# Ten weight pairs instead of eight of the second half's second layer by seven products, with joins and weight differences in other slots

## The chip, the cores and the metric

The kernel runs on one core of one Trainium2 chip. The metric is device time in microseconds (us). Five engines work side by side, each with its own in-order queue: TensorE (PE in the profile; its weight loads are PEld), VectorE (DVE), ScalarE (ACT), GpSimd (POOL) and SyncE (SP), which here issues all DMAs. L893 is line 893 of the kernel.

## The reference

One layer norm feeds two branches, and both are added to the input. All values are float32.

```python
S, D, F = 2048, 576, 4608          # tokens, width, hidden width
xn = layernorm(x)
# A: 32 heads of 18, each token looks at itself and 7 earlier ones, 2 apart
q, k, v = split(xn @ wqkv)
o = softmax(q . k[pos - 2 w], w = 0..7) . v
# B: Dense -> Mish -> Dense
act = mish(xn @ w1 + b1)
y = act @ w2
out = x + o @ wo + y
```

## The kernel before

**Numbers.** Each float32 operand of a matrix product is split into a high part (a ScalarE copy to the type fp32r) and a low part (the rest, a subtraction on VectorE or GpSimd). A product is three matmuls: high by high, high by low, low by high.

**Halves, blocks, weight pairs.** The 2048 tokens are two halves of 1024 (`hf`), each half two blocks of 512 (`b`), each block four tiles of 128. The hidden width is 36 slices of 128; two slices make a weight pair `q`, 0 to 17. In the second half the slices are taken in the order `Q1`. `m1_part(hf, q, part)`, parts 0 to 5, computes the first layer of a weight pair for both blocks by seven products (lines 680 and 686), and `mish` makes the activations: an addition on VectorE where the product is a sum of two (L725), Mish on ScalarE (L726), a high copy (L731) and a low part on GpSimd (L732).

**The second layer, two forms.** In the first half `m2_pair` (L780) and in the second `m2_cols` (L893) multiply the activations of one weight pair with its two slices of w2 and add the result to the accumulators. One call is a chunk: two token tiles, two column halves of 288, 24 matmuls. A weight pair has four chunks, in the order of `CHUNKS`: block 1 twice, block 0 twice. Each of the four results of a chunk lies in one of the four PSUM banks called `out`, and VectorE adds it to its accumulator (L784, L896), which frees the bank.

The other form is used in the second half for weight pairs 1 to 2 x `OC`, two pairs at a time (`e`, from 0 to `OC` - 1). The two blocks of tokens and the two column halves make a 2 x 2 product, done by seven products instead of eight (Strassen and Winograd's scheme). `p_item(e, k)` is one of the seven, in the order `ORD` = P7, P4, P1, P5, P2, P6, P3; it has 24 matmuls (L872). Its left side is an activation or a sum of activations (`u_sum`, L814), split by `u_high` (L820) and `u_low` (L826); its right side is a quarter of w2 or a difference of quarters, kept in DRAM by the first half and brought by `p_fetch` (L840). For that the first half makes the differences T3, T1, T2, T4 of each such weight pair (`t_sum`, L301), splits them (`t_high` L307, `t_low` L312) and stores them (`t_keep`, L322 and L323). Each product has an accumulator of its own over all `e`, two tiles each (`accP1` to `accP7`); VectorE adds to it (L878). P2, P3, P4 and P5 start from the input x. When the last seven are done, `p_join` (L881, GpSimd) adds accumulators to each other, 14 additions of 128 x 576, so that P2, P3, P4 and P5 become the four quarters of the output, to which the remaining chunks add directly.

In the second half, position q of the order has weight pair `Q1[q]` = q + 1 (the last position has 0). The names of slots, `spot(1, q, i)`, and the table `early` go by position, so that `early[16]` and `early[17]` are the last two weight pairs. Positions 0 to 2 x `OC` hold their activations unsplit in buffers given by `raw_act`, since the sums are made of them; position 2 x `OC` is the first whose second layer goes by chunks, and `a_split` (L834, L835) splits what it holds.

**The order.** The program is a list `plan` of steps: attention projections, parts of `m1_part`, products, chunks, and at the end the output projection. `quad(hf, q)` writes one weight pair's steps; ten such steps of a pair are named by `spot(hf, q, i)`, i from 0 to 9. `before(i, fn)` hangs further work in front of step i. Engines get their instructions in exactly this order, and nothing is moved later.

**Attention** of a half is a generator of 73 steps: per pair of head groups four multiplies q by k on GpSimd (L539, two instructions) with a reduction on VectorE (L544), one softmax step, four multiplies by v (L577) with a reduction (L583). The reduction of a step is issued in the next step, so that GpSimd has time. After the last one VectorE transposes (L603) and SP stores to DRAM (L612). `cuts[hf]` lists the steps of the plan that carry an attention step. In the first half they follow from estimated costs at a spacing in `t`; in the second half from the table `early` (three slots a weight pair where products run, five else), cut off at 73, which today puts the last two of them on the first two of the final four chunks. Where a step is in `behind_adds` or `behind_next`, its reduction goes behind the additions of that step or the next.

**Other work in the queues.** The second half's part of the attention projection is also done by seven products; its weights (names beginning with z: `z_load` L385, `z_sum`, `z_high`, `z_low`, `z_keep`) are prepared in the first half in tiles of the pool `xn`, which has five and which the differences T use too. `wo_load`, `wo_sum`, `wo_keep_high` and so on prepare the output projection's weights in the second half. In the output projection (`wo_part`, L1076) each pair of token tiles is split by `o_split` (L924 to L955), the first of them during the last chunks, and VectorE adds the results (L1080).

Of the kernel before, what the change touches and what calls it, by code (L numbers as in the profile page):

```python
# [28 lines left out]
UQ = 4  # L29
PU = 2  # L30
CU = 2 * DH
OC = 4
Q1 = [*range(1, NP), 0]
HC = D // 2
EPS = 1e-5
# [4 lines left out]
def block_kernel(ctx: ExitStack, tc: tile.TileContext, x, wq, wo, w1, b1, w2, mask, out):  # L40
# [469 lines left out]
    behind_adds, behind_next, now = set(), set(), [0]  # L510
# [181 lines left out]
    def raw_act(q, b, j):  # L692
        if not rslot:
            for n in range(4):
                rslot["raw", n] = sb.tile([P, 5 * P], F32, tag="raw", bufs=4, name=f"ra{n}")
            for n in range(5):
                rslot["mn", n] = sb.tile([P, D], F32, tag="mn", bufs=5, name=f"rm{n}")
            for n in range(2):
                rslot["tt", n] = sb.tile([P, 4 * P], F32, tag="tt", bufs=2, name=f"rt{n}")
        tag, n = {(0, 0): (("raw", 0), ("raw", 1), ("raw", 2)), (1, 0): (("mn", 2), ("mn", 3), ("mn", 0), ("r3", 0)),  # L700
                  (0, 1): (("raw", 3), ("mn", 4), ("mn", 1)), (1, 1): (("tt", 0), ("tt", 1))}[b, j][q % {(1, 0): 4, (1, 1): 2}.get((b, j), 3)]
        if (tag, n) not in rslot:
            rslot[tag, n] = sb.tile([P, 2 * 432], F32, tag="r3", bufs=1, name="ra_r")
        rawact[q, b, j] = rslot[tag, n][:, 0:TB]
        owner[tag, n] = q, b, j
        where[q, b, j] = tag, n
        return rawact[q, b, j]
# [448 lines left out]
    at = {}  # L1156
# [26 lines left out]
    items = []  # L1183
# [172 lines left out]
    def spot(hf, q, i):  # L1356
        return at["s", hf, q, i]

    for q in range(NP):
        if q == 0:  # L1360
            i = at["q", 0, 3, 1, 0]
            ps_ = dict(raw=i - 3, sums=i - 1, wa=i, wc=i + 1, t0=i + 2, t1=i + 4)
        elif q == 1:
            i = at["q", 0, 3, 0, 0]
# [16 lines left out]
    for q in range(1, 2 * OC + 1):  # L1381
        i = spot(0, q, (3,2)[q > 1])
# [5 lines left out]
    i = spot(0, NP - 1, 0)  # L1388
# [5 lines left out]
    i = at["q", 1, 0, 1, 1]  # L1394
    for name, k, d in (("T2", 0, 0), ("T2", 1, 1), ("T3", 0, 2), ("B11", 0, 3), ("B11", 1, 4), ("B21", 0, 5),
                       ("B21", 1, 6), ("R2", 0, 7), ("T3", 1, 8), ("R3", 0, 9), ("T1", 0, 10), ("T1", 1, 10),
                       ("T4", 0, 11), ("T4", 1, 11), ("B22", 0, 11), ("B22", 1, 11)):
        before(i + d, lambda name=name, k=k: z_fetch(name, k))
    i = spot(0, 9, 4)
    for k in range(2):  # L1400
        for n, steps in enumerate((
# [4 lines left out]
            for kind, name in steps:  # L1406
                f = dict(l=z_load, s=z_sum, h=z_high, o=z_low, k=z_keep)[kind]
                d = 30 + 2 * n + (n >= 14) if k else 2 * n if n < 10 else (19, 20, 22, 23, 25, 26, 27)[n - 10]
                before(i + d, lambda f=f, name=name, k=k: f(name, k))
    for q in range(NP):  # L1410
        if q == 0:
            i = at["z", JB - 1, 0]
            ps_ = dict(wa=i - 7, t0=i - 6, t1=i - 5, wc=i - 4)
        elif q == 1:
            i = spot(1, 0, 0)
# [22 lines left out]
    J = 2 * OC + 1  # L1438
    for b in range(NB):
        for j in range(2):  # L1440
            before(spot(1, J, 0) + (2,3,1,2)[2 * b + j], lambda b=b, j=j: a_split(b, j))
    for n, (a, b) in enumerate((("P6", "P1"), ("P7", "P6"), ("P6", "P5"), ("P2", "P1"), ("P3", "P6"), ("P4", "P7"), ("P5", "P7"))):
        for pr in range(2):
            i = items[-2][2] + 1 + (0,1,2)[n] if n < 3 else at["p", 1, J + 0 - 1, n > 4, pr] + (1, 7, 1, 2)[n - 3]
            before(i, lambda a=a, b=b, pr=pr: p_join(a, b, pr))

    i = at["q", 0, 1, 1, 0]
# [3 lines left out]
    i = at["q", 0, 3, 1, 0]  # L1451
# [5 lines left out]
    i = at["q", 1, 0, 1, 1]  # L1457
    for n in range(8):
        c, k = divmod(n, 4)
        d = i + (0, 1, 3, 4, 6, 8, 10, 12)[n]  # L1460
        before(d, lambda c=c, k=k: s_step(1, c, k))
        d = max(d + 2, (at["q", 1, 1, 1, 2], at[("z", 1, 2)])[c] if k == 3 else 0)
# [4 lines left out]
    for n in range(0, JB, 2):  # L1467
        i = at["q", 0, 1, 0, n]
# [4 lines left out]
    for n in range(TJ):  # L1473
        i = spot(0, 2 + n, 2)
# [3 lines left out]
    i = spot(0, NP - 2, 0)  # L1478
# [7 lines left out]
    for n, (name, pr) in enumerate((name, pr) for name in ("P4", "P5", "P2", "P3") for pr in range(2)):  # L1486
        i = items[dict(P4=0, P5=2, P3=2, P2=3)[name]][2] + pr
# [2 lines left out]


    att = {}
    behind_adds.update((at["p", "x", OC - 1, 4], at["p", "x", 0, 4]))
    behind_next.add(at["m", 1, 10, 3])
    T = [0.0]
    for p_ in plan:
        T.append(T[-1] + p_[2])
# [15 lines left out]
    cuts = [[], []]  # L1513
    k = marks[0] - 1
    for n in range(steps - len(last_steps)):
        t = 6.111 * n
        k = next(k for k in range(k + 1, len(plan)) if T[k + 1] > t and ok[k])
        cuts[0].append(k)
    cuts[0] += last_steps
    early = {0: (8,), 1: (0, 2, 4, 6, 8), 2: (0, 4, 7), 3: (0, 3, 6), 4: (0, 4, 7), 5: (0, 3, 7), 6: (1, 4, 7),  # L1520
             7: (0, 4, 7), 8: (1, 4, 8), 9: (1, 3, 7)}
    for q in range(NP):
        cuts[1] += [spot(1, q, i) for i in early.get(q, (1, 3, 5, 7, 9))]
        if q == 2 * OC:
# [6 lines left out]
        for k in cuts[hf]:  # L1531
            before(k, lambda hf=hf: next(att[hf], None))

    i = spot(1, *(11,3))
    for k in range(4):
        before(i - 8 + 2 * k, lambda k=k: wo_load(k))
    for n in range(4):
        before(i + (0,2,4,6)[n], lambda n=n: wo_sum(n))
    for n, name in enumerate(("T3", "T1", "T2", "T4", "B11", "B21", "B22", "R", "D")):
        k = i + 10 + (2, 5, 10, 15, 20, 25, 30, 35, 40)[n]  # L1540
        if name == "R":
            before(k - 8, lambda: wo_rest(0))
        before(k, lambda name=name, n=n: wo_keep_high(name, n))
        before(k + 1, lambda name=name: wo_keep_low(name))
        before(k + 2, lambda name=name: wo_keep(name))
    i = spot(1, NP - 1, 0)
# [71 lines left out]
```

## Time and profile before

| | us |
|---|---|
| median of 3 runs (lowest to highest) | 1112.72 (1112.7 to 1113.13) |
| the profiled execution | 1113.35 |
| its span | 1111.6 |
| TensorE busy | 1101.6 |
| VectorE busy | 850.2 |
| GpSimd busy | 789.8 |
| ScalarE busy | 498.9 |

A page gives busy time by engine, the chain of work that ended last, and groups of instructions with their count, busy time, mean duration and the idle time of the engine in front of them. The timeline has a row for each group of equal instructions: start, length, engine, line, operation, tiles, count, and in brackets how long the engine was idle in front of it and who ended that. Matmuls are pipelined: neighbours overlap in these rows, so distances between starts are what counts. In the chain, rows are start, length, what. The windows view gives busy time and count of PE, PEld, DVE, ACT and POOL in a stretch, then clock, DMA share and GB/s. The last matmul of the first half's second layer (L780) starts at 545.5 us; the products (L872) start between 654.3 and 824.2; the second half's chunks (L893) start between 827.0 and 1053.8, and the output projection follows.

### The profile page before, as it was taken

How to read it: one execution, taken by the hardware profiler on the slowest of the kernel's cores; microseconds unless marked ns; L12 is line 12 of the kernel's file. 1: busy time of each engine (PE TensorE's matmuls, PEld its weight loads, DVE VectorE, ACT ScalarE, POOL GpSimd, SP SyncE). 2: the span in 40 equal slices, each digit the busy share in tenths (PEclk: the TensorE clock that was granted, in tenths of full speed). 3: DMA queues.
4: the chain of work that ended last, by engine and by line, in shares of the span. 5: the costliest groups of instructions: out<-in, count | busy, mean ns of one | idle time of the engine just before them, and what ended most of it. 6: DMA issues, size and time to landing. Idle time of an engine off the chain costs nothing.

```text
span 1111.6 us, 18209 instructions
## 1 busy us (share of the span) xinstructions
PE 1101.6 (99%) x6550; PEld 1014.5 (91%) x6550; DVE 850.2 (76%) x1367; ACT 498.9 (45%) x917; POOL 789.8 (71%) x639
## 2 busy tenths in 40 slices
PE   8999999999999999999999999999999999999998
PEld 7999899999999999999999888999888999999998
DVE  6359788888889888897656567877876677777786
ACT  5544655544454544555333354443432344343353
POOL 2479777766779688685788666666688976867542
PEclk9999999999999999999999999999999999999999
DMA  6899696868777768675598799656674657776674
GB/s 200 284 311 312 231 346 225 282 237 274 255 247 263 264 212 298 249 255 201 187 322 268 225 378 304 214 189 207 219 230 161 210 195 214 245 284 219 183 233 142
DMA packets 178270, 271.60 MB, mean 244 GB/s; under 512 B 53218, under 2 KB 120068, under 8 KB 178180
## 3 DMA queue, kind: packets, MB, share of 16 engines
q1 hardware_dynamic: 178180, 270.44, 72.3%
q8 instruction: 52, 0.85, 0.3%
q14 instruction: 38, 0.31, 0.1%
HBM read 160.39 MB, written 110.00 MB: 243 GB/s over the span
## 4 chain that ended last, share of the span: by engine, by line
PE 90%; DMA 4%; DVE 2%; POOL 1%; ACT 1%; SPq 1%; issue 1%; POOLq 0%; DVEq 0%
PE h L680 27%; PE po L780 21%; PE pq L348 11%; PE po L893 11%; PE po L872 6%; PE h L686 5%; PE o L1076 5%; PE z L446 3%; DMA acc<-in_x 1%; DMA kv<-kv_d 1%; DMA t<-kept_t 1%; DMA accP<-in_x 1%; SPq L612 1%; POOL act L732 1%; DMA pw<-kept_T 1%
## 5 line engine op out<-in xcount | busy, mean ns | idle before, releaser
L780 PEld LDWEIGHTS po<-w,act 128*128 128x128 f32 x1728 | 236.4, 188 | 6.0 <-POOL act L732 0.4
L780 PE MATMUL po<-w,act 128*128 128x288 f32 x1728 | 240.7, 295 | 0.1
L539 POOL TENSOR_TENSOR pr<-q,kv 128x576 f32<-128x576 f32 x128 | 197.3, 1566 | 8.1 <-DMA q<-q_d 4.9
L732 POOL TENSOR_TENSOR act<-c,act 128x512 fp32r<-128x512 f32 x81 | 107.4, 1327 | 128.5 <-ACT act L731 127.9
L577 POOL TENSOR_TENSOR pv<-L,kv 128x576 f32<-128x576 f32 x128 | 178.4, 1488 | 24.8 <-DVE L L570 19.9
L784 DVE TENSOR_TENSOR acc<-po,acc 128x288 f32<-128x288 f32 x288 | 119.5, 449 | 29.9 <-PE po L780 28.8
L348 PE MATMUL pq<-wq,xt 128*128 128x432 f32 x672 | 136.4, 361 | 1.1 <-ACT xt L81 1.1
L893 PEld LDWEIGHTS po<-w,act 128*128 128x128 f32 x960 | 130.9, 188 | 5.9 <-DVE accP L896 3.0
L893 PE MATMUL po<-w,act 128*128 128x288 f32 x960 | 133.3, 295 | 2.4 <-DVE accP L896 2.4
L348 PEld LDWEIGHTS pq<-wq,xt 128*128 128x128 f32 x672 | 125.0, 188 | 8.1 <-ACT xt L81 1.9
L726 ACT ACTIVATE c<-c,b1c 128x512 f32<-128x512 f32 x81 | 58.7, 725 | 140.9 <-DVE c L725 140.6
L680 PE MATMUL h<-xt,t 128*128 128x512 f32 x432 | 110.6, 391 | 0.7 <-DVE rt L725 0.7
L680 PE MATMUL h<-S,t 128*128 128x512 f32 x432 | 110.5, 391 | 0.0
L583 DVE TENSOR_REDUCE og<-pv 128x144 f32<-128x1152 f32 x64 | 85.9, 1345 | 23.9 <-POOL pv L577 23.8
L680 PE MATMUL h<-xt,wa 128*128 128x512 f32 x432 | 104.1, 390 | 0.0
L544 DVE TENSOR_REDUCE L<-pr 128x64 f32<-128x1152 f32 x64 | 85.8, 1342 | 23.3 <-POOL pr L539 23.2
L714 ACT COPY c<-h 128x512 f32<-128x512 f32 x81 | 47.4, 586 | 124.5 <-PE h L686 73.4
L680 PEld LDWEIGHTS h<-xt,wa 128*128 128x128 f32 x432 | 80.9, 188 | 17.0
L872 PEld LDWEIGHTS po<-pw,u 128*128 128x128 f32 x672 | 91.9, 188 | 3.8 <-DVE accP L878 1.3
L872 PE MATMUL po<-pw,u 128*128 128x288 f32 x672 | 94.1, 295 | 0.5 <-DVE accP L878 0.3
L680 PEld LDWEIGHTS h<-xt,t 128*128 128x128 f32 x432 | 79.1, 188 | 15.6 <-DVE rt L725 1.2
L896 DVE TENSOR_TENSOR accP<-po,accP 128x288 f32<-128x288 f32 x160 | 69.0, 452 | 31.7 <-PE po L893 29.0
(228 smaller groups left out, 1852.1 us busy)
## 6 DMA issues: line engine op xcount, KB each, us to landing
kv<-kv_d SPq DMA_DIRECT2D x64, 396.0 KB, 4.8
kept_t<-t SPq DMA_DIRECT2D x36, 512.0 KB, 4.8
t<-kept_t SPq DMA_DIRECT2D x36, 512.0 KB, 6.4
rw<-in_w SPq DMA_DIRECT2D x36, 320.0 KB, 4.8
kept_wa<-wa SPq DMA_DIRECT2D x18, 640.0 KB, 4.9
kept_w<-w SPq DMA_DIRECT2D x20, 576.0 KB, 4.2
wa<-kept_wa SPq DMA_DIRECT2D x18, 640.0 KB, 5.2
w<-kept_w SPq DMA_DIRECT2D x20, 576.0 KB, 4.1
```

The lines of the kernel that those rows point to most:

```text
L348: nc.tensor.matmul(pq[:, 0:432], XT[:, xi, tok], wt[wi][:, hl, 0:432], start=i == 0, stop=i == len(seq) - 1)
L539: nc.gpsimd.tensor_tensor(out=pr[:, x:x + hh], in0=q[:, j0 + x:j0 + x + hh, None, :].to_broadcast([P, hh, W, CU]), in1=win(kt, 0, CU, j0 + ...
L544: nc.vector.tensor_reduce(L[:, k, j0:j0 + hj].rearrange("p j w h -> p (j w h)"), pr.rearrange("p j w (h d) -> p (j w h) d", h=2), axis=AX, ...
L577: nc.gpsimd.tensor_tensor(out=pr[:, x:x + hj].rearrange("p j d w -> p j w d"), in0=L[:, k, x:x + hj, :, h:h + 1].to_broadcast([P, hj, W, DH]),
L583: nc.vector.tensor_reduce(og[:, c0:c0 + DH, :].rearrange("p d j -> p j d"), pr, axis=AX, op=ALU.add)
L680: nc.tensor.matmul(ph, wt[:, wl, wk * P:(wk + 1) * P], X[:, xs, :], start=first and i == 0, stop=last and i == len(seq) - 1, skip_group_ch ...
L732: nc.gpsimd.tensor_tensor(out=a[:, 1, :], in0=t, in1=a[:, 0, :].bitcast(F32), op=ALU.subtract)
L780: nc.tensor.matmul(po, acts[hf, q, b, j][:, al, tok], done["w2", hf, 2 * q + j][:, wl, c * HC:(c + 1) * HC], start=i == 0, stop=i == 5)
L784: nc.vector.tensor_tensor(out=t, in0=po, in1=t, op=ALU.add)
L872: nc.tensor.matmul(po, units[e, k, qq][:, al, tok], w[:, qq, wl, :], start=i == 0, stop=i == 5)
L893: nc.tensor.matmul(po, acts[hf, q, b, j][:, al, tok], done["w2", hf, 2 * q + j][:, wl, c * HC:(c + 1) * HC], start=i == 0, stop=i == 5)
L896: nc.vector.tensor_tensor(out=t, in0=po, in1=t, op=ALU.add)
```

## The change

`OC` becomes 5: weight pairs 9 and 10 go from chunks to a fifth set of seven products, and the first half prepares their weight differences. The joins get other slots, and P3 += P5 in front of the last product replaces P6 += P5; the sums are the same. One reduction loses its place behind additions. The preparation of the z weights, the attention steps of both halves and the output projection's weights get other slots, and one held activation another buffer.

```diff
@@ -29,7 +29,7 @@
-OC = 4
+OC = 5
@@ -698,7 +698,7 @@ raw_act
         tag, n = {(0, 0): (("raw", 0), ("raw", 1), ("raw", 2)), (1, 0): (("mn", 2), ("mn", 3), ("mn", 0), ("r3", 0)),
-                  (0, 1): (("raw", 3), ("mn", 4), ("mn", 1)), (1, 1): (("tt", 0), ("tt", 1))}[b, j][q % {(1, 0): 4, (1, 1): 2}.get((b, j), 3)]
+                  (0, 1): (("raw", 3), ("mn", 4), ("mn", 1)), (1, 1): (("tt", 0), ("tt", 1))}[b, j][3 if (q, b, j) == (2 * OC, 1, 0) else q % {(1, 0): 4, (1, 1): 2}.get((b, j), 3)]
@@ -1396,7 +1396,7 @@
-    i = spot(0, 9, 4)
+    i = spot(0, 10, 6)
     for k in range(2):
         for n, steps in enumerate((
...
                 f = dict(l=z_load, s=z_sum, h=z_high, o=z_low, k=z_keep)[kind]
-                d = 30 + 2 * n + (n >= 14) if k else 2 * n if n < 10 else (19, 20, 22, 23, 25, 26, 27)[n - 10]
+                d = 28 * k + (2 * n if n < 10 else (19, 20, 22, 23, 25, 26, 27)[n - 10])
@@ -1439,9 +1439,11 @@
-    for n, (a, b) in enumerate((("P6", "P1"), ("P7", "P6"), ("P6", "P5"), ("P2", "P1"), ("P3", "P6"), ("P4", "P7"), ("P5", "P7"))):
-        for pr in range(2):
-            i = items[-2][2] + 1 + (0,1,2)[n] if n < 3 else at["p", 1, J + 0 - 1, n > 4, pr] + (1, 7, 1, 2)[n - 3]
+    last = at["p", "x", OC - 1, 5]
+    for pr in range(2):
+        for a, b, i in (("P3", "P5", last), ("P6", "P1", last + 1), ("P7", "P6", last + 3),
+                        ("P2", "P1", at["p", 1, J - 1, 0, pr] + 1), ("P3", "P6", at["p", 1, J - 1, 0, pr] + 7),
+                        ("P4", "P7", at["p", 1, J - 1, 1, pr] + 1), ("P5", "P7", at["p", 1, J - 1, 1, pr] + 2)):
             before(i, lambda a=a, b=b, pr=pr: p_join(a, b, pr))
@@ -1490,8 +1492,8 @@
-    behind_adds.update((at["p", "x", OC - 1, 4], at["p", "x", 0, 4]))
-    behind_next.add(at["m", 1, 10, 3])
+    behind_adds.add(at["p", "x", OC - 1, 4])
+    behind_next.add(at["m", 1, 2 * OC + 2, 3])
@@ -1513,12 +1515,13 @@
-        t = 6.111 * n
+        t = 5.95 * n
...
     early = {0: (8,), 1: (0, 2, 4, 6, 8), 2: (0, 4, 7), 3: (0, 3, 6), 4: (0, 4, 7), 5: (0, 3, 7), 6: (1, 4, 7),
-             7: (0, 4, 7), 8: (1, 4, 8), 9: (1, 3, 7)}
+             7: (0, 4, 7), 8: (1, 4, 7), 9: (0, 4, 7), 10: (1, 4, 8), 11: (1, 3, 7),
+             16: (0, 2, 4, 5, 7, 9), 17: (0, 2, 4, 5, 7, 9)}
@@ -1531,13 +1534,13 @@
-    i = spot(1, *(11,3))
+    i = spot(1, 13, 0)
     for k in range(4):
         before(i - 8 + 2 * k, lambda k=k: wo_load(k))
...
     for n, name in enumerate(("T3", "T1", "T2", "T4", "B11", "B21", "B22", "R", "D")):
-        k = i + 10 + (2, 5, 10, 15, 20, 25, 30, 35, 40)[n]
+        k = i + 10 + (2, 5, 8, 12, 15, 19, 23, 27, 31)[n]
```

With the new table the 73 attention steps of the second half end on the last of the final four chunks.

## The prediction

> **What bounds the kernel now.** I read the page first: engine totals, chain by engine, costliest groups.
>
> ```profile
> span 1111.6 us, 18209 instructions
> PE 1101.6 (99%) x6550; PEld 1014.5 (91%) x6550; DVE 850.2 (76%) x1367; ACT 498.9 (45%) x917; POOL 789.8 (71%) x639
> PE 90%; DMA 4%; DVE 2%; POOL 1%; ACT 1%; SPq 1%; issue 1%; POOLq 0%; DVEq 0%
> L893 PE MATMUL po<-w,act 128*128 128x288 f32 x960 | 133.3, 295 | 2.4 <-DVE accP L896 2.4
> L872 PE MATMUL po<-pw,u 128*128 128x288 f32 x672 | 94.1, 295 | 0.5 <-DVE accP L878 0.3
> ```
>
> TensorE is busy 99% of the span and is 90% of the chain that ended last. So a matmul removed is time removed, and work of other engines counts only where TensorE waits for it. L893 is the eight-product form in the second half, L872 the seven-product form. Next the chain in order of time, for what one unit of either costs:
>
> ```profile
> 710.83 3.20 PE po L872 x24
> 877.03 3.18 PE po L893 x24
> 901.11 3.18 PE po L893 x24
> ```
>
> A chunk of L893 and a product of L872 are both 24 matmuls and 3.18 to 3.20 us, 132.5 ns a matmul. The same chunk of the next weight pair comes 24.08 us later: that is a pair's period where nothing waits.
>
> Then I looked in the timeline for the places where TensorE does wait. The largest is the change from products to chunks (TensorE):
>
> ```profile
> 821.14 3.33 PE L872 MATMUL po<-pw,u 128*128 128x288 f32 x24
> ...
> 831.58 0.61 PE L686 MATMUL h<-xt,wc 128*128 128x512 f32 x2
> 833.85 1.85 PE L893 MATMUL po<-w,act 128*128 128x288 f32 x12 [1.66 <-DVE accP L896]
> ...
> 838.13 1.54 PE L680 MATMUL h<-xt,t 128*128 128x512 f32 x6
> ```
>
> The two L686 matmuls take 0.46 (they overlap), the chunk 3.18, so the next L680 was due at 835.22. It started at 838.13: 2.91 us lost. VectorE and then GpSimd at that place say why:
>
> ```profile
> 832.08 1.35 DVE L544 TENSOR_REDUCE L<-pr 128x64 f32<-128x1152 f32 x1 [7.11 <-POOL pr L539]
> 835.91 0.82 DVE L896 TENSOR_TENSOR accP<-po,accP 128x288 f32<-128x288 f32 x2 [1.75 <-POOL accP L881]
> ```
> ```profile
> 818.92 1.29 POOL L835 TENSOR_TENSOR act<-rm,act 128x512 fp32r<-128x512 f32 x1 [3.67 <-ACT act L834]
> ...
> 829.23 2.81 POOL L539 TENSOR_TENSOR pr<-q,kv 128x576 f32<-128x576 f32 x2
> ...
> 834.46 2.79 POOL L881 TENSOR_TENSOR accP<-accP,accP 128x576 f32<-128x576 f32 x2
> ```
>
> VectorE stood 7.11 us in front of an attention reduction whose multiply (L539) ran on GpSimd behind two joins of P7; the adds that empty the first chunk's PSUM banks stood behind it. The second pair of these adds then waited 1.75 for the join P6 += P5, which reads the accumulator they write. With no bank free, TensorE waited.
>
> **One chunk less.** Weight pairs 9 and 10 of the second half cost 2 x 4 chunks today and 7 products after the change. That removes 24 matmuls: -3.18 us, all on TensorE's path. [...]
>
> **The change from products to chunks** moves two pairs later, with other joins. P3 += P5 replaces P6 += P5 and stands one product ahead of the last. By the product before the last, P5 is complete, and GpSimd has 3.67 us idle there (row 818.92) for the 2.79 us of this pair. P7 += P6 goes behind the attention multiply, not in front. So, on the old clock, GpSimd comes to the multiply at about 826.5 and ends it at 829.3. VectorE reduces until about 830.7 and the first bank is free near 831.2, while the chunk is due at 832.04. The wait on P6 += P5 has no successor: P5's readers are done. Taken: the whole 2.91 goes. Bounds: 0 to -2.91; I take the upper end because the cover is 0.8 us and GpSimd's queue ahead of the multiply is 2.8 us shorter. Next late is the VectorE queue two chunks on, with a cover of about 1.9 us. Later joins (P4, P5, P2, P3) stay behind their adds, as now.
>
> **The end of the second half's attention.** It loses slots in weight pairs 10 and 11 and gets six instead of five in 16 and 17, and its last steps go to the last two chunks, not the two before. The built program's order on VectorE shows what this puts between the last chunks: a reduction L583 where the transpose L603 was, another L583 in front of the last four adds, and L603 behind L952, in front of the first L1080. Today there (VectorE, TensorE, GpSimd):
>
> ```profile
> 1045.62 1.36 DVE L583 TENSOR_REDUCE og<-pv 128x144 f32<-128x1152 f32 x1 [0.59 <-POOL pv L577]
> ...
> 1049.01 0.77 DVE L603 STREAM_TRANSPOSE oT<-og 128x576 f32<-128x576 f32 x1
> ...
> 1052.70 0.69 DVE L948 TENSOR_TENSOR oa<-ot,oa 128x512 fp32r<-128x512 f32 x1 [0.65 <-ACT oa L944]
> ...
> 1055.21 0.43 DVE L952 TENSOR_TENSOR ob<-ot,ob 64x256 fp32r<-64x256 f32 x1
> 1055.66 1.05 DVE L1080 TENSOR_TENSOR y<-o,y 128x288 f32<-128x288 f32 x2
> ```
> ```profile
> 1053.90 1.76 PE L1076 MATMUL o<-wo,oa 128*128 128x288 f32 x12
> 1055.69 0.54 PE L1076 MATMUL o<-wo_r,ob 128*128 128x288 f32 x2
> 1056.18 1.85 PE L1076 MATMUL o<-wo,oS 128*128 128x288 f32 x12
> ```
> ```profile
> 1041.73 1.30 POOL L732 TENSOR_TENSOR act<-mn,act 128x512 fp32r<-128x512 f32 x1 [2.54 <-ACT act L731]
> 1042.99 2.59 POOL L577 TENSOR_TENSOR pv<-L,kv 128x576 f32<-128x576 f32 x2
> ```
>
> TensorE already runs at VectorE's heels here: its matmul at 1055.69 comes 0.05 behind the end of L952, that at 1056.18 just behind the first of the two L1080 (1055.66 + 0.45). Two more L583 in this queue, 2 x 1.27 (1.36 less the 0.08 by which neighbours overlap), push both by about 2.5 us. GpSimd's three remaining multiplies end at about 45.6, 48.2 and 50.8 on this clock, ahead of their reductions, and add nothing. The output projection behind this is as dense as the rest and gives nothing back: +2.5 us. Bounds 0 (if VectorE were ahead, which the rows exclude) to 3.5 (GpSimd's pairs taking 3.7, below).
>
> **Smaller steps on the path.** In the first seven products, a reduction no longer goes behind the adds of the fifth product. Today (VectorE, TensorE):
>
> ```profile
> 684.99 1.54 DVE L878 TENSOR_TENSOR accP<-po,accP 128x288 f32<-128x288 f32 x4
> 686.45 1.34 DVE L544 TENSOR_REDUCE L<-pr 128x64 f32<-128x1152 f32 x1
> ...
> 688.91 0.68 DVE L725 TENSOR_TENSOR rt<-h,rt 128x512 f32<-128x512 f32 x1
> ```
> ```profile
> 685.49 3.44 PE L872 MATMUL po<-pw,u 128*128 128x288 f32 x24 [0.30 <-DVE accP L878]
> 689.65 1.66 PE L680 MATMUL h<-xt,t 128*128 128x512 f32 x6 [0.71 <-DVE rt L725]
> ```
>
> With the two swapped, the product at 685.49 starts 1.26 later and ends near 689.95. What follows waited until 689.65 for L725 anyway, so 0.3 us remains. Bounds 0 to 1.26.
>
> The new fifth set of seven brings VectorE and GpSimd low parts and sums of u, of which the tightest is the last product's, with a join beside it:
>
> ```profile
> 811.53 3.72 POOL L539 TENSOR_TENSOR pr<-q,kv 128x576 f32<-128x576 f32 x2
> ```
> ```profile
> 812.05 1.91 DVE L814 TENSOR_TENSOR rm<-rm,ra_r 128x512 f32<-128x512 f32 x1
> ...
> 819.45 1.31 DVE L826 TENSOR_TENSOR u<-ra,u 128x512 fp32r<-128x512 f32 x1
> ```
>
> L826 ends at 820.76, and the product using it starts at 821.14 without a wait. The extra pair of joins can hold it by one join, 1.4 (half of 2.79); bounds 0 to 1.4, taken 0.2, as VectorE has other work to do meanwhile.
>
> **The first half at nothing.** Weight pairs 9 and 10 get four differences, two high and two low copies and more, smaller transfers each, as pairs 1 to 8 have; the preparation of the z weights starts 12 slots later; attention's spacing goes from 6.111 to 5.95. The cover is that TensorE never waits there, with VectorE almost full:
>
> ```profile
> 333.60:361.40 27.80, 27.80 (x166) 25.26 (x165) 25.74 (x34) 12.60 (x21) 25.82 (x20) 1.00 0.78 264
> ```
>
> (DVE 25.74 and POOL 25.82 of 27.80, PE 27.80.) A new wait stands in SP's queue: the three z loads now come right behind the kept T3 of pair 10 and need its buffers, so SP stands for one landing, and the w1 loads behind it with it. Today (SP, GpSimd, and the landing of these loads):
>
> ```profile
> 347.81 1.85 SPq L199 DMA_DIRECT2D rw<-in_w  x2
> ```
> ```profile
> 359.14 1.11 POOL L240 TENSOR_TENSOR tt<-rw,rw 128x256 f32<-128x256 f32 x1
> ```
> ```profile
> DMA to landing us min/median/max: 2.8/5.0/7.2
> ```
>
> Issued by 349.7, landed by 354.7, used at 359.14: 4.4 us of slack against a delay of about 5. GpSimd would wait under 1 us, and the casts behind it are used a weight pair later. Taken 0; if that cover failed, 1 us.
>
> **The sum** on the profiled execution: -3.18 - 2.91 + 2.5 + 0.3 + 0.2 = -3.1, and I round to -2.9 for a tenth or two of new small waits in the fifth set. The profiled execution took 1113.35 (span 1111.6), 0.63 over the median of the runs, 1112.72; both move alike. Forecast: 1110.4 in a profile, **1109.8** as median. What a measurement can tell from no change is about 0.2%, 2.2 us.
>
> **Rivals.**
> A, the wait at the change from products to chunks only changes its name. For it: the same in-order queues, four casts, fourteen joins and attention in one stretch, and 0.8 us of cover. Against: the rows' order above. The sum loses its 2.91: 1112.7.
> B, the last chunks hide the two reductions. For it: VectorE idles in parts of the last 30 us. Against: 1055.69 and 1056.18 follow VectorE. The sum loses the 2.5: 1107.3.
> C, the joins hold VectorE out. The row 812.05 is 1.91 for a shape that takes 0.68 at 688.91 with a PSUM operand, while GpSimd ran the 3.72 us pair. If P3 += P5 does that to the sums and low parts of the last two products, one join is added: 1.4, so 1111.2. [...]
> D, slower: six attention steps in a weight pair overrun GpSimd in pairs 16 and 17. A pair of multiplies takes 2.59 to 3.72 (rows 1042.99, 811.53), the four casts 4 x 1.30. At 3.72 this is 6 x 3.72 + 5.2 = 27.5 us in a period of 24.08: 3.4 over, twice, and the reductions hold the chunk adds behind them. The sum becomes -2.9 + 6.8: 1116.6. It decides from 3.15 us a pair upward. Against: 2.59 to 2.81 in rows 829.23 and 1042.99.
>
> **How the numbers follow.** Forecast 0.45, A 0.2, B 0.13, C 0.14, D 0.08. Faster by over 0.2%: forecast, B and a third of C, 0.63. Within 0.2%: A and the rest of C, 0.29. Slower: D, 0.08. The range reaches from B to A, 1107.3 to 1112.7, and leaves out D and the tails; the forecast's own range is 1108.6 to 1111.0.
>
> **What would show it.** Right: 840 matmuls at L872 and 768 at L893; no idle bracket over 0.5 at the first chunks behind the products; TensorE's first L1076 rows with the third some 4.8 us behind the first (2.28 now), L952 and L1080 ending just before; nothing new before 640 us. A: a bracket at L893 from VectorE, with VectorE waiting for L577 or L881. B: the distance stays 2.3. C: L814 and L826 near 1.9 beside L881, a bracket at the last product. D: brackets at L893 in the last 60 us. A wait in the first half would make the forecast wrong outright.

## The result: 15.4 us slower

| kernel | median, us | runs | lowest to highest |
|---|---|---|---|
| before | 1112.93 | 4 | 1112.7 to 1113.2 |
| changed | 1128.35 | 4 | 1127.73 to 1129.19 |

The ratio is 1.0137 (95% interval 1.0125 to 1.015). The forecast was 1109.8, with a range of 1107.3 to 1112.7 and "faster" as the likeliest. It was wrong in sign and size. The profiled execution of the changed kernel took 1129.19 us.

The page of the changed kernel: engine totals, chain by engine, and the two groups of the second layer.

```profile
span 1127.4 us, 18203 instructions
PE 1104.9 (98%) x6526; PEld 1015.1 (90%) x6526; DVE 850.8 (75%) x1381; ACT 502.6 (45%) x927; POOL 794.0 (70%) x647
PE 79%; DVE 7%; POOL 6%; DMA 3%; issue 3%; ACT 2%; SPq 0%; DVEq 0%; POOLq 0%
L872 PE MATMUL po<-pw,u 128*128 128x288 f32 x840 | 117.4, 295 | 1.8 <-DVE accP L878 1.8
L893 PE MATMUL po<-w,act 128*128 128x288 f32 x768 | 107.4, 296 | 0.0
```

24 matmuls fewer, as intended. But TensorE's share of the chain fell from 90% to 79%: more of the chain now runs through VectorE (7% after 2%) and GpSimd (6% after 1%). Both hardly work more (VectorE 850.8 us after 850.2, GpSimd 794.0 after 789.8). So the loss is not an engine that became the bound. It is TensorE's waiting: of the 15.8 us between the two spans 12.5 are time in which TensorE was not busy, and its busy time rose by 3.3 in spite of the matmuls removed, since its clock was lower for a while (mean granted clock 0.994 after 1.000; last section).

To find where, I take the starts of the same matmuls in both traces (the view of one line's instructions; "120.5 to 545.5" are the first and the last start). Before, then changed:

```profile
L780 PE MATMUL po<-w,act x1728: 288/295/402, 120.5 to 545.5; 128*128 128x288 f32 x192
L872 PE MATMUL po<-pw,u x672: 290/294/402, 654.3 to 824.2; 128*128 128x288 f32 x168
L893 PE MATMUL po<-w,act x960: 288/294/398, 827.0 to 1053.8; 128*128 128x288 f32 x192
```
```profile
L780 PE MATMUL po<-w,act x1728: 288/295/403, 120.5 to 549.6; 128*128 128x288 f32 x192
L872 PE MATMUL po<-pw,u x840: 288/294/402, 666.0 to 881.9; 128*128 128x288 f32 x168
L893 PE MATMUL po<-w,act x768: 288/294/442, 884.8 to 1065.9; 128*128 128x288 f32 x192
```

These marks cut the span into four stretches (the start, 120 us, is the same everywhere). Each entry is a difference of two such starts in the one profiled execution; the last is the span's end less the last start of L893. The same is done for all experiments, whose table below uses these names:

| us | first half | projection | second half | end | median of runs |
|---|---|---|---|---|---|
| before | 425.0 | 108.8 | 399.5 | 57.8 | 1112.93 |
| changed | 429.1 | 116.4 | 399.9 | 61.5 | 1128.35 |
| difference | +4.1 | +7.6 | +0.4 | +3.7 | +15.4 |

The four differences add up to the 15.8 us between the two spans. The forecast gave 0 to the first two, -5.6 to the third, and +2.5 to the last. Three places hold most of the loss. The 4.1 us of the first half are spread: TensorE waits 0.65, 0.57 and 1.21 us, near 130, 207 and 393 us, where it waited less than 0.05 before, and no single wait shows for the rest.

**The attention projection, 7.6 us.** TensorE, VectorE and GpSimd of the changed kernel:

```profile
598.86 0.55 PE L446 MATMUL z<-z_R,xt 128*128 128x432 f32 x2
604.63 2.53 PE L446 MATMUL z<-z_B,S 128*128 128x432 f32 x6 [5.22 <-DVE zqs L459]
```
```profile
596.89 0.68 DVE L666 TENSOR_TENSOR S<-s,S 128x512 fp32r<-128x512 f32 x1
602.64 1.35 DVE L583 TENSOR_REDUCE og<-pv 128x144 f32<-128x1152 f32 x1 [5.07 <-POOL pv L577]
603.91 0.45 DVE L459 TENSOR_TENSOR zkv<-z,zkv 128x288 f32<-128x288 f32 x1
```
```profile
597.65 1.30 POOL L630 TENSOR_TENSOR s_u<-xt,xt 128x512 f32<-128x512 f32 x1 [0.92 <-DVE S L666]
599.02 1.26 POOL L630 TENSOR_TENSOR s<-s,s_u 128x512 f32<-128x512 f32 x1
600.25 2.36 POOL L577 TENSOR_TENSOR pv<-L,kv 128x576 f32<-128x576 f32 x2
```

VectorE stood for 5.07 us in front of a reduction (L583) whose multiply (L577) ran on GpSimd behind two sums for the next products (L630), the first of which in turn waited for VectorE. The additions that free the projection's PSUM banks (L459) stood behind that reduction, and TensorE waited 5.22. In the kernel before, the multiply stood ahead of these sums:

```profile
589.00 3.01 POOL L577 TENSOR_TENSOR pv<-L,kv 128x576 f32<-128x576 f32 x2
591.84 1.33 POOL L630 TENSOR_TENSOR s<-xt,xt 128x512 f32<-128x512 f32 x1
594.08 1.30 POOL L630 TENSOR_TENSOR s_u<-xt,xt 128x512 f32<-128x512 f32 x1 [0.91 <-DVE S L666]
595.45 1.29 POOL L630 TENSOR_TENSOR s<-s,s_u 128x512 f32<-128x512 f32 x1
```

Nothing was added there. With a spacing of 5.95 the first half's attention comes into the projection one step behind. Of the four parts (0 to 3) of each token tile in the last stretch of the projection, the steps lay on 1 3, 1 3, 1 3, 1 before, and now on 1 2, 0 2, 0 2, 0 2. The wait itself is 5.22; the rest of the 7.6 is a lower clock behind it (0.55 and 0.59 in the windows from 602 to 610, last section).

**The seam of weight pairs 16 and 17, some 5 us.** The wait is in pair 17, the last of the order. TensorE, VectorE, GpSimd:

```profile
1041.39 1.80 PE L680 MATMUL h<-xt,t 128*128 128x512 f32 x6 [3.11 <-DVE c L725]
```
```profile
1021.67 0.76 DVE L977 TENSOR_TENSOR rwo_r<-rwo_r,woh_R 128x576 fp32r<-128x576 f32 x1 [2.98 <-POOL wo_d L973]
...
1039.38 1.35 DVE L544 TENSOR_REDUCE L<-pr 128x64 f32<-128x1152 f32 x1 [1.40 <-POOL pr L539]
1040.65 0.68 DVE L725 TENSOR_TENSOR c<-h,c 128x512 f32<-128x512 f32 x1
```
```profile
1033.78 8.30 POOL L539 TENSOR_TENSOR pr<-q,kv 128x576 f32<-128x576 f32 x6
```

The steps on the places 2, 4 and 5 of pair 17 put three multiplies in a row on GpSimd, 8.30 us; in the old order a low part of an activation (L732) stood between any two of these. Two of their reductions (L544) stand in front of L725, which TensorE's next product needs. Behind the wait of 3.11 the next 32 matmuls took 6.7 us instead of 5.0 (granted clock 0.79 and 0.64 in the two 3-us windows from 1041 on).

**The end, 3.7 us.** TensorE, the third L1076 row is now 4.61 behind the first (2.28 before), with L952 and L1080 (VectorE) ending just ahead of the waiting matmuls:

```profile
1066.00 1.76 PE L1076 MATMUL o<-wo,oa 128*128 128x288 f32 x12
1069.32 0.54 PE L1076 MATMUL o<-wo_r,ob 128*128 128x288 f32 x2 [1.56 <-DVE ob L952]
1070.61 3.13 PE L1076 MATMUL o<-wo,oS 128*128 128x288 f32 x12 [0.76 <-DVE y L1080]
```

**What did come.** The change from products to chunks no longer waits (TensorE):

```profile
884.77 3.34 PE L893 MATMUL po<-w,act 128*128 128x288 f32 x24
887.94 1.53 PE L680 MATMUL h<-S,t 128*128 128x512 f32 x6
889.31 0.62 PE L686 MATMUL h<-xt,wc 128*128 128x512 f32 x2
889.77 3.34 PE L893 MATMUL po<-w,act 128*128 128x288 f32 x24
892.94 1.53 PE L680 MATMUL h<-xt,t 128*128 128x512 f32 x6
```

### The profile page after: what moved, and what is told of

Its sections match the earlier page's. It is cut to its first block, busy times and chain, and to the rows that moved or that the text cites. A ratio compares the mean times of both kernels' runs of the same rounds, so it can differ in the third digit from the quotient of the medians.

```text
span 1127.4 us, 18203 instructions
## 1 busy us (share of the span) xinstructions
PE 1104.9 (98%) x6526; PEld 1015.1 (90%) x6526; DVE 850.8 (75%) x1381; ACT 502.6 (45%) x927; POOL 794.0 (70%) x647
## 4 chain that ended last, share of the span: by engine, by line
PE 79%; DVE 7%; POOL 6%; DMA 3%; issue 3%; ACT 2%; SPq 0%; DVEq 0%; POOLq 0%
PE h L680 24%; PE po L780 18%; PE pq L348 11%; PE po L872 8%; PE o L1076 5%; PE h L686 5%; PE po L893 4%; PE z L446 3%; POOL pv L577 3%; POOL pr L539 1%; POOL act L732 1%; DVE L L544 1%; DMA kv_d<-kvs 1%; DVE w L255 1%; DMA t<-kept_t 1%
## 5 line engine op out<-in xcount | busy, mean ns | idle before, releaser
L780 PEld LDWEIGHTS po<-w,act 128*128 128x128 f32 x1728 | 236.3, 188 | 8.3 <-DVE acc L784 2.6
L780 PE MATMUL po<-w,act 128*128 128x288 f32 x1728 | 241.1, 295 | 1.5 <-DVE acc L784 1.2
L577 POOL TENSOR_TENSOR pv<-L,kv 128x576 f32<-128x576 f32 x128 | 176.5, 1475 | 28.3 <-DVE L L570 21.0
L732 POOL TENSOR_TENSOR act<-c,act 128x512 fp32r<-128x512 f32 x75 | 99.3, 1325 | 122.2 <-ACT act L731 105.0
L872 PEld LDWEIGHTS po<-pw,u 128*128 128x128 f32 x840 | 115.0, 188 | 5.7 <-DVE accP L878 2.7
L872 PE MATMUL po<-pw,u 128*128 128x288 f32 x840 | 117.4, 295 | 1.8 <-DVE accP L878 1.8
L726 ACT ACTIVATE c<-c,b1c 128x512 f32<-128x512 f32 x75 | 54.4, 725 | 141.8 <-DVE c L725 141.3
L583 DVE TENSOR_REDUCE og<-pv 128x144 f32<-128x1152 f32 x64 | 86.1, 1346 | 34.0 <-POOL pv L577 33.9
L893 PEld LDWEIGHTS po<-w,act 128*128 128x128 f32 x768 | 105.9, 190 | 2.5
L893 PE MATMUL po<-w,act 128*128 128x288 f32 x768 | 107.4, 296 | 0.0
L544 DVE TENSOR_REDUCE L<-pr 128x64 f32<-128x1152 f32 x64 | 85.8, 1343 | 19.7 <-POOL pr L539 19.6
L680 PEld LDWEIGHTS h<-S,t 128*128 128x128 f32 x432 | 77.9, 188 | 13.6 <-ACT rm L714 0.5
L714 ACT COPY c<-h 128x512 f32<-128x512 f32 x75 | 43.9, 586 | 96.9 <-PE h L686 50.7
```

Of the source, the lines that this page charges most:

```text
L544: nc.vector.tensor_reduce(L[:, k, j0:j0 + hj].rearrange("p j w h -> p (j w h)"), pr.rearrange("p j w (h d) -> p (j w h) d", h=2), axis=AX, ...
L577: nc.gpsimd.tensor_tensor(out=pr[:, x:x + hj].rearrange("p j d w -> p j w d"), in0=L[:, k, x:x + hj, :, h:h + 1].to_broadcast([P, hj, W, DH]),
L583: nc.vector.tensor_reduce(og[:, c0:c0 + DH, :].rearrange("p d j -> p j d"), pr, axis=AX, op=ALU.add)
L680: nc.tensor.matmul(ph, wt[:, wl, wk * P:(wk + 1) * P], X[:, xs, :], start=first and i == 0, stop=last and i == len(seq) - 1, skip_group_ch ...
L732: nc.gpsimd.tensor_tensor(out=a[:, 1, :], in0=t, in1=a[:, 0, :].bitcast(F32), op=ALU.subtract)
L780: nc.tensor.matmul(po, acts[hf, q, b, j][:, al, tok], done["w2", hf, 2 * q + j][:, wl, c * HC:(c + 1) * HC], start=i == 0, stop=i == 5)
```

## The experiments

The times on the right are medians, the stretches come from one profiled execution of each kernel, so differences of some tenths between them mean little. Each kernel was timed beside the kernel before, whose median was 1112.8 to 1113.5 in these sets.

| run | first half | projection | second half | end | median, us | ratio to before, 95% interval |
|---|---|---|---|---|---|---|
| e1 first half's old slots | 431.6 | 108.8 | 404.3 | 60.2 | 1125.01 | 1.0095 to 1.0125 |
| e2 end's steps to pairs 12 to 15 | 429.0 | 116.4 | 403.4 | 57.9 | 1129.41 | 1.0134 to 1.0165 |
| e3 old joins | 429.0 | 116.7 | 401.8 | 61.7 | 1130.89 | 1.0148 to 1.0178 |
| e4 eight pairs, new joins | 425.0 | 108.6 | 396.3 | 57.9 | 1110.02 | 0.9966 to 0.9985 |
| e5 e4 and the new slots | 429.7 | 115.1 | 397.9 | 60.2 | 1125.72 | 1.0097 to 1.0131 |
| e6 ten pairs, other slots | 427.8 | 108.8 | 407.8 | 57.9 | 1124.65 | 1.0085 to 1.0115 |
| e7 earlier wo weights | 429.5 | 115.2 | 402.2 | 61.7 | 1129.56 | 1.0123 to 1.016 |
| e8 ten pairs, best slots | 428.4 | 108.7 | 401.5 | 57.9 | 1118.06 | 1.0025 to 1.0057 |
| e9 e4 and one reduction | 424.9 | 108.8 | 396.6 | 57.8 | 1110.18 | 0.9967 to 0.9991 |
| e10 four steps left out | 427.9 | 108.6 | 397.2 | 57.9 | 1113.21 | 0.9992 to 1.0011 |
| e11 and no new differences | 425.0 | 108.7 | 398.8 | 57.9 | 1110.40 | 0.9968 to 0.9986 |

**The joins: e3 and e4.** e3 is the changed kernel with the old joins, e4 the kernel before with the new ones (the diff is e4's):

```diff
-    for n, (a, b) in enumerate((("P6", "P1"), ("P7", "P6"), ("P6", "P5"), ("P2", "P1"), ...
+    last = at["p", "x", OC - 1, 5]
+    for pr in range(2):
+        for a, b, i in (("P3", "P5", last), ("P6", "P1", last + 1), ("P7", "P6", last + 3), ...
```

> The changed kernel with the old joins in their old slots (P6 += P5 in place of P3 += P5, all behind the product before the last). Theory (the join wait is gone): TensorE's wait of 2.5 to 2.9 us at the change from products to chunks comes back there, and the 1.1 us wait in front of the product at 859 stays: about 1131. Rival (it had only changed its name, or another order of attention did it): within 1 us of the changed kernel, 1128.

> The kernel before, eight weight pairs by products, with the new joins in the new slots and nothing else. Theory: the 2.9 us at the change from products to chunks go, and up to 1 us of it comes back where the joins hold VectorE at the last product: 1110 to 1111. Rival (joins lock VectorE out or the wait changes its name): 1112.5 or more.

Both came as expected. In e3 the two waits are back (TensorE), and the kernel is 2.5 us slower than the changed one; e4 is 2.8 us faster than the kernel before, and no other run is faster than it.

```profile
891.83 1.85 PE L893 MATMUL po<-w,act 128*128 128x288 f32 x12 [1.35 <-DVE accP L896]
894.31 1.86 PE L893 MATMUL po<-w,act 128*128 128x288 f32 x12 [0.64 <-DVE accP L896]
```

**The first half's slots: e1.** The changed kernel with

```diff
-    marks = [..., spot(0, 2 * OC + 1, 0), at["q", 1, 0, 0, 0],
+    marks = [..., spot(0, 9, 0), at["q", 1, 0, 0, 0],
-        t = 5.95 * n
+        t = 6.111 * n
```

> The changed kernel with the first half's attention on the same steps as in the kernel before (spacing 6.111, the sparse stretch ending at weight pair 9); all else as changed, the differences of weight pairs 9 and 10 included. Theory (places of the reductions): TensorE's 5.4 us stall in the attention projection goes, with the lowered clock behind it, 7.5 us in all, and about 4 us of small stalls at 129, 206 and 391 us: some 1117 us. Rival (work): the first half cannot take the differences of pairs 9 and 10 beside four attention steps a pair; VectorE and GpSimd overrun there, by 3 us or more at 330 to 400 us, and the time stays above 1119.

Each was half right. The projection is back to 108.8, so there it was the slots. But the first half got longer, 431.6. In weight pair 9, with four attention steps and its differences, TensorE waited for this (TensorE, VectorE, GpSimd):

```profile
327.39 2.37 PE L680 MATMUL h<-xt,t 128*128 128x512 f32 x6 [2.32 <-DVE c L725]
```
```profile
325.98 0.76 DVE L312 TENSOR_TENSOR twT<-twT,twhT 128x576 fp32r<-128x576 f32 x1 [2.59 <-ACT twhT L307]
```
```profile
321.25 3.34 POOL L577 TENSOR_TENSOR pv<-L,kv 128x576 f32<-128x576 f32 x2
324.44 0.80 POOL L301 TENSOR_TENSOR twT<-rw,twT 128x288 f32<-128x288 f32 x1
```

An attention multiply stands in front of the last difference (L301), its copy (ScalarE, L307) and low part (L312) come late, and L725 stands behind L312. So the old slots are dearer beside the new work, and the new ones have a price in the projection. The second half of e1 has the same order as the changed kernel's and yet took 4.4 us longer; part of it is a wait of 1.84 at 876.51 (last section). The profiled execution, 1126.81, was the longest of e1's four.

**The slots alone: e5.** e4 with spacing 5.95, the sparse stretch to pair 11, and four steps of pairs 10 and 11 moved to 16, 17 and the last two chunks; no fifth set, old slots for the weights:

```diff
-             7: (0, 4, 7), 8: (1, 4, 8), 9: (1, 3, 7)}
+             7: (0, 4, 7), 8: (1, 4, 8), 9: (1, 3, 7), 10: (1, 4, 8), 11: (1, 3, 7),
+             16: (0, 2, 4, 5, 7, 9), 17: (0, 2, 4, 5, 7, 9)}
```

> The kernel before with the new joins and with the attention steps of both halves where the change puts them (spacing 5.95 with the sparse stretch to weight pair 11; four steps taken from the second half's pairs 10 and 11 and given to 16 and 17 and the last two chunks); eight weight pairs by products, old slots for the z and output projection weights. Base without these slots: 1110.0. Theory (the places alone cost the time): the stall in the attention projection comes back with 7.5 us, those at 129 and 206 with 2 us, and pairs 16 and 17 and the last chunks cost 9 us: about 1128. Rival (it is the work of the fifth set and of the moved weight preparations beside the steps): the first half stays at 1110 and the end costs 2.5 us or less: 1110 to 1113.

15.7 us more than e4 (15.0, if each is taken against the kernel before in its own set), without any of the new work: first half +4.7, projection +6.5, second half +1.6, end +2.3. The first half's waits are near the same places as in the changed kernel (0.62, 0.59 and 0.84 us). So the places alone account for most of the loss. The seam is the exception: here its three multiplies start in time, and TensorE waits only 0.26 (GpSimd, TensorE):

```profile
1031.90 8.34 POOL L539 TENSOR_TENSOR pr<-q,kv 128x576 f32<-128x576 f32 x6
```
```profile
1039.51 1.63 PE L680 MATMUL h<-xt,t 128*128 128x512 f32 x6 [0.26 <-DVE c L725]
```

**The seam: e7 and e2.** e7 moves the last weight preparations of the output projection out of pair 17, e2 the four attention steps:

```diff
-        k = i + 10 + (2, 5, 8, 12, 15, 19, 23, 27, 31)[n]
+        k = i + 10 + (2, 4, 6, 9, 11, 14, 17, 20, 24)[n]
```
```diff
-             16: (0, 2, 4, 5, 7, 9), 17: (0, 2, 4, 5, 7, 9)}
+             12: (1, 3, 5, 7, 8, 9), **dict.fromkeys((13, 14, 15), (1, 2, 4, 6, 7, 9))}
```

> The changed kernel with the last of the output projection's weight preparations closer together, so that they end in weight pair 16 where the kernel before ended them, and not in 17. Theory (GpSimd's and VectorE's pieces of that preparation in pair 16 hold VectorE's addition and with it GpSimd's cast, so that three attention multiplies start 2.9 us late and TensorE waits 3.3 us at the seam of pairs 16 and 17): the stall near 1038 falls below 0.5 and the window around it loses 4.5 us: about 1124. Rival (the three multiplies in a row at the seam are too many by themselves): within 1 us of the changed kernel.

> The changed kernel with six attention steps in weight pairs 12 to 15 of the second half and five in 16 and 17, so that the last two steps fall on the first two of the last four chunks, as before. Theory (places at the seam of pairs 16 and 17 and on the last chunks): the stall of 3.3 us near 1038 and those of 1.7 and 0.9 near 1067 go, with their lowered clock 8.5 us: about 1120. Rival (amount): six steps a pair are too many for GpSimd anywhere behind the products, and the 8.5 us turn up in pairs 12 to 15: no change, 1128.

In e7 the wait at the seam fell to 0.27, so its cause is shown: the preparation (row 1021.67 above: VectorE waits 2.98 for GpSimd's piece) made the three multiplies late. But the time did not fall, since a moved piece made a wait of 3.34 earlier: VectorE stood 2.18 us in front of it for GpSimd, behind it came a softmax step, and only then the additions that free the banks. In e2 the wait at the seam fell to 0.76 and those at the end are gone, and the rival was right: the steps cost as much where they went, 2.81 in pair 13 and 1.27 in pair 14. VectorE and TensorE in e7, then TensorE in e2:

```profile
1005.47 1.83 DVE L977 TENSOR_TENSOR rwo_r<-rwo_r,woh_R 128x576 fp32r<-128x576 f32 x1 [2.18 <-POOL wo_d L973]
```
```profile
1011.35 3.01 PE L893 MATMUL po<-w,act 128*128 128x288 f32 x11 [3.34 <-DVE accP L896]
```
```profile
939.32 4.97 PE L893 MATMUL po<-w,act 128*128 128x288 f32 x24 [2.81 <-DVE accP L896]
```

**Other slots for everything: e6 and e8.** Ten pairs, the first half's steps by a list written out (two a pair up to pair 8, old places in the projection). e6 puts the second half's four steps under the products, where GpSimd stands idle for 3.5 to 7.6 us at a time; e8 uses e7's offsets, moves two steps of the list, keeps six steps in 16 and 17, puts one more in pair 0 and one in pair 15, and moves the entry of `behind_next` one part ahead (the diff is e6's):

```diff
-    cuts[0] += last_steps
+    cuts[0] = [21, 22, 24, ..., 249, 251, 253] + last_steps
-             7: (0, 4, 7), ..., 16: (0, 2, 4, 5, 7, 9), 17: (0, 2, 4, 5, 7, 9)}
+             7: (0, 4, 7), 8: (1, 4, 7), 9: (0, 4, 7), 10: (1, 4, 8), 11: (1, 3, 7)}
+    cuts[1] += [at["p", "x", 0, 5], at["p", "x", 1, 5], at["p", "x", 2, 2], at["p", "x", 3, 5]]
```

> The changed kernel with the first half's steps by a list (two a pair to pair 8, then a mixture, and on the old steps of the attention projection), and in the second half four more steps under the products (items 5, 5, 2 and 5 of the first four sets) in place of those added to pairs 16 and 17, so that the end is as in the kernel before. Theory (a place has to have room on VectorE and GpSimd; idle GpSimd gaps of 3.5 to 7.6 us stand beside the products): the 7.5 us, the 4 us of the first half down to 1 to 2, and the 9 us of the end all go, with up to 2 us of new waits under the products: 1109 to 1111. Rival (no place has room: every step added to any pair costs some 2 us): 1117 or more.

> Ten weight pairs with all that the runs so far point to: the first half's steps by a list with two steps moved, the earlier output projection weights, one attention step more in pair 0 and one in pair 15 of the second half, so that the last two steps fall on the first two of the last four chunks. Theory (room exists at some places): 1110 for eight pairs with the new joins, less 3.2 for the product, plus 1 to 3 of small waits: 1108 to 1110, faster than both kernels. Rival (each step that is moved costs some 2 us wherever it goes): 1113 or more.

Both missed. The projection's loss goes in both, the first half keeps 2.8 to 3.4, the end has no wait, and the second half is longer than before: +8.3 in e6, +2.0 in e8. Idle gaps of GpSimd were no room: VectorE was busy for all of the 6 us from 689 to 695. In e6 the additional reduction stood in front of L725 (VectorE, TensorE):

```profile
691.90 1.89 DVE L814 TENSOR_TENSOR rm<-ra,rm 128x512 f32<-128x512 f32 x1
693.72 1.34 DVE L544 TENSOR_REDUCE L<-pr 128x64 f32<-128x1152 f32 x1
694.98 0.67 DVE L725 TENSOR_TENSOR rt<-h,rt 128x512 f32<-128x512 f32 x1
```
```profile
695.71 1.58 PE L680 MATMUL h<-xt,t 128*128 128x512 f32 x4 [3.20 <-DVE rt L725]
```

**One reduction: e9.** e4 with the reduction at the fifth of the first seven products in front of the additions.

```diff
-    behind_adds.update((at["p", "x", OC - 1, 4], at["p", "x", 0, 4]))
+    behind_adds.add(at["p", "x", OC - 1, 4])
```

> Eight weight pairs, new joins, and the reduction at the fifth of the first seven products in front of the additions, as the change has it; nothing else. Base 1110.0. Theory: 0.3 us more (bounds 0 to 1.26): 1110.3. Rival (it also holds the next product): 1111 or more.

1110.18 against 1110.02: no difference that can be measured, so neither 0 nor 0.3 is excluded. In the profile the product now waits 1.32 in front, and the wait of 0.69 that e4 has for the next L725 is gone (TensorE):

```profile
686.39 3.47 PE L872 MATMUL po<-pw,u 128*128 128x288 f32 x24 [1.32 <-DVE accP L878]
```

**Ten pairs with work left out: e10 and e11.** e10 has e6's first half and leaves four attention steps out, e11 also leaves out the new differences and has the first half of the kernel before:

```diff
-            for k, vt in enumerate(vs):
+            less = hf == 1 and pair >= 6
+            ...
+            for k, vt in enumerate(vs[:1] if less else vs):
```
```diff
-    for q in range(1, 2 * OC + 1):
+    for q in range(1, 9):
...
-        nc.sync.dma_start(t.bitcast(F32), kept[name, e])
+        nc.sync.dma_start(t.bitcast(F32), kept[name, min(e, 3) if name[0] == "T" else e])
```

> Ten weight pairs, the first half's steps by the first list, and four attention steps of the second half left out: in its last two pairs of head groups the second multiply by v and its reduction are not done, for both column parts (the output lacks them). The table then has five steps in every pair from 12 on and the end of the kernel before. Theory (the fifth set takes four places from the attention, and it is their work that finds no room): nothing above 1 us is left in the products and behind them, and the time is 1110.0 - 3.2 for the product + 2.5 for the first half + up to 3 for the fifth set's own waits near 690, 790 and 857: 1110 to 1113. Rival (the fifth set's own work and the later weight preparations overload pairs 10 to 17 even so): 1116 or more.

> The one before, and the four differences of weight pairs 9 and 10 are not made and not stored; the fifth set multiplies by those of the fourth (the output has these in their place); the first half's attention and z weights in the slots of the kernel before. Theory: the first half returns to no wait at all, 2.5 to 3 us less than the run with four steps left out, and the product saved shows at last: 1107 to 1110. Rival (the fifth set costs in the second half what it saves): 1111 or more.

e10 came 0.2 above the theory's range, e11 0.4 above its own. Even with the four steps and the differences for nothing, ten pairs take as long as eight with the same joins (1110.40 and 1110.02). The second half should be 3.2 below e4's 396.3, at 393.1; it is 397.2 and 398.8 (the profiled e11 took 1112.86, the longest of its runs, so part of its 5.7 is not typical). TensorE's longest waits there are 1.88, 0.95 and 0.81 us in e11 (near 687, 850 and 1030), where e4 has one of 0.69. The first (L874 is the product here):

```profile
687.17 4.96 PE L874 MATMUL po<-pw,u 128*128 128x288 f32 x24 [1.88 <-DVE accP L880]
```

All three stand behind a reduction of the attention (L544), which stands in front of the additions or of the next L725. The first is no matter of the fifth set: e9 has it with eight pairs, 1.32. e10 and e11 keep the new places of the other attention steps and of the output projection's weights, so what the fifth set's own work costs, and what these places cost, is not separated.

## Why the prediction was wrong

**One chunk less: right, and not enough.** 840 and 768 matmuls, 24 fewer. e10 and e11 show that the second half as rearranged for the fifth set gives all of it back in waits, even with four attention steps left out. The forecast had allowed "a tenth or two" for that.

**The change from products to chunks: right.** 2.91 forecast; 2.8 in e4, 2.5 in e3.

**The end of the attention: mechanism right, price low.** The third L1076 was forecast 4.8 behind the first and came 4.61 behind. But this stretch lost 3.7, not 2.5, since TensorE's clock fell after the wait: 0.67 and 0.76 in the two 3-us windows from 1069 on. In e1 and e5 the third row comes as late (4.7 and 4.6 behind the first), but no matmul of L1076 took longer than 0.40 us (0.61 in the changed kernel), and the end is 60.2, 2.4 above the kernel before: the forecast's price is that of the waits alone.

**Rival D, 0.08: the wrong place for the price.** It compared the work of a whole weight pair with its period, and found room at 2.8 us a multiply. One such multiply did take 2.77 (8.30 / 3). What decided was the order within 10 us: three in a row at the seam behind a late low part. e7 shows the other half of the cause, the moved weight preparation, which the prediction didn't cost.

**"The first half at nothing": the step that failed.** It is 11.7 us (4.1 and 7.6) of the 15.8 us by which the spans differ, and the forecast's sign "nothing new before 640 us" failed with it. The prediction costed the differences and the z loads, and dealt with the new spacing in half a sentence. Its cover, "TensorE never waits there", was read in the kernel before and says only that the old order has no wait. It also looked at weight pairs only, not at the projection, where steps of the same attention run. There each step came one behind. e5 shows the loss with no new work at all (4.7 and 6.5), and e1, e6 and e8 that the projection's part of it goes with other places. The second half fell short as well: +0.4 where -5.6 was forecast, of which the seam is some 5.

**The small steps.** +0.3 at the first set: e9, nothing measurable. +0.2 at the last product: it has no wait at all (878.81); the product at 859.09 waits 0.97 for additions behind a reduction and a softmax step of the attention instead. Rival C, joins that hold VectorE out, did not show in the changed kernel's time; in e1 one subtraction beside joins took 4.25 us, below.

What stays open: whether some other order brings ten pairs below e4. e8 was the nearest tried that leaves nothing out, 8 us away.

## What to carry to other kernels

A step that is moved in in-order queues is costed at its new place, by what stands behind its wait there. That the old place was free, or that an engine's average has room, did not tell it here. Where one parameter moves a whole series of steps, list where each of them lands before and after, over the whole kernel, and not only where the work changes. Where an engine is busy 99% of the time, an order of its helpers has been found that fits: before giving it up for 3 us, try the part of the change that moves nothing else. Here that is the joins alone, e4: 1110.02 us, faster than both kernels.

## What the runs showed of the hardware

A wait of TensorE can cost more than its length: the stretch with the 5.22 us lost 7.6. With this wait, up to 604.63, the granted clock (the number behind the five engines) was 0.55 and 0.59 in the windows from 602 to 610:

```profile
602.00:606.00 4.00, 1.37 (x4) 1.29 (x5) 3.36 (x7) 0.00 (x0) 4.00 (x4) 0.55 0.00 0
606.00:610.00 4.00, 4.00 (x15) 3.68 (x14) 1.07 (x1) 0.81 (x3) 4.00 (x4) 0.59 0.73 102
610.00:614.00 4.00, 4.00 (x22) 3.83 (x21) 1.93 (x3) 1.22 (x5) 1.38 (x2) 1.00 0.97 340
```

Of the 7.6 us, 5.4 were lost up to the matmul at 604.63 and 2.2 behind it. A shorter wait can do it too: behind 1.88 us in e11 a product took 4.96 us in place of 3.3 (granted clock 0.60 and 0.83 in the two 3-us windows from 687 on), while behind 0.97 in the changed kernel it took 3.44 (1.00 in the two 3-us windows from 858 on). The length alone does not settle it, though. In e10 a wait of 1.78 (in front of 689.65) left the clock at 1.00 in the four 3-us windows from 686 on. In e6, behind 2.80 (in front of 745.56), the next six matmuls took 1.65 us, about as long as behind 0.26 in e5 (1.63, row 1039.51 above), where six took 1.80 behind 3.11 in the changed kernel. And the shorter waits at the end, 1.56 and 0.76, had 0.67 and 0.76 behind them in the changed kernel, while in e1 and e5, with the third row as late, the longest matmul of L1076 took 0.40 us (0.61 in the changed kernel). What settles it, no run here shows.

One operation of VectorE took far longer beside GpSimd's joins than elsewhere. In e1 a subtraction (L826) that takes 0.68 to 1.72 us in the changed kernel (0.68 at 698.73) took 4.25, beside a pair of joins and a low part behind them on GpSimd. The next L826 came late, and the product that needs it waited 1.84 (VectorE, GpSimd, TensorE):

```profile
869.45 4.25 DVE L826 TENSOR_TENSOR u<-ra,u 128x512 fp32r<-128x512 f32 x1
```
```profile
869.03 2.87 POOL L881 TENSOR_TENSOR accP<-accP,accP 128x576 f32<-128x576 f32 x2
871.80 1.35 POOL L835 TENSOR_TENSOR act<-ra_r,act 128x512 fp32r<-128x512 f32 x1
```
```profile
876.51 4.70 PE L872 MATMUL po<-pw,u 128*128 128x288 f32 x22 [1.84 <-DVE u L826]
```
